# Attention with top-32 masking and routed experts on one core: a new order of emission, and value products of the shared tile that alternate between the heads

## The chip, the core and the metric

The kernel runs on one core of one Trainium2 chip. A core has TensorE (PE in the profile; its weight loads are shown as PEld), VectorE (DVE), ScalarE (ACT), GpSimd (POOL) and SyncE (SP), which here issues DMAs. Each engine works off its own queue of instructions in the order in which the program emitted them, and waits on semaphores for the others. The metric is device microseconds of one execution, here the median of three runs.

## The reference

For 8 batches of 8 heads, with 576 rows of 64, attention keeps for each row the scores that are not below the 32nd largest:

```python
scores = scale * np.matmul(q, k.transpose(0, 1, 3, 2))
kth = np.partition(scores, -top_k, axis=-1)[..., -top_k:-top_k + 1]
mask = scores >= kth
scores = np.where(mask, scores, -1000000000.0)
...
attn = attn / (np.sum(attn, axis=-1, keepdims=True) + 1e-09)
return np.matmul(attn, v).astype(np.float32)
```

Its output, 4608 tokens of 512, goes through a router with 8 experts. Tokens are assigned greedily by descending logit, each expert takes at most 576, and each expert is a product with w1, a ReLU and a product with w2.

## The kernel before, in words

The kernel has two parts, one behind the other: `attention` and `moe`. Only `attention` is touched by the change. It works through 32 pairs of heads (8 batches with 4 pairs each). A pair has 9 tiles of 128 query rows: tiles 0 to 3 are of the first head, 5 to 8 of the second, and tile 4, the shared tile, holds the last 64 rows of both heads, one on partitions 0 to 63 and one on 64 to 127.

One tile goes through this chain. TensorE forms scores in PSUM tile `s` (L216, four matmuls; three such tiles exist). VectorE takes the eight largest of each of six chunks of 96 (L219), and from these 48 candidates the 24 largest in five steps (L222 to L226: MAX, MATCH_REPLACE, MAX, MATCH_REPLACE, MAX). L227 forms a bias from the 24th, ScalarE writes a sign mask `w` and its count (L231). TensorE adds `w` times a huge number into `s` (L234 with `off`, a matmul of 512 columns and one of 64), before which VectorE fills 8 spare columns (L237). VectorE finds the next eight, ranks 25 to 32 (L238). TensorE takes the huge number out again (L234 with `back`), and ScalarE's ReLU turns scores into the mask tile `r` (L241), which frees `s` for the tile after the next two.

A second chain, later in time, goes from `r` to the output. TensorE lays mask and scores into PSUM tile `pt`, keys on partitions (L279, L284, L285), ScalarE takes the exponential `F` (L289), and GpSimd splits it into two fp16 halves, `ehm` (L292) and `elm` (L295). The value products (L363) sum these against `vh` and `vl`, twelve fp16 matmuls for each tile and one fp32 matmul for the last 64 keys (`E4`). The shared tile is not split: each head of it has four fp32 matmuls with `E` and one with `E4r`, with a weight of 64 columns, so that head 0 writes partitions 0 to 63 of `pv` and head 1 partitions 64 to 127. VectorE forms row sums and their reciprocal (L343, L377), ScalarE scales (L345).

Once for each pair GpSimd prepares the operands of a coming pair: q and k are scaled (L175), cut into high and low halves (L177, L178, L179), v is scaled (L167, L168), ScalarE makes its high half `vh` (L169), and GpSimd the low half `vl` (L170). SP issues the loads (L156, L157, L162, L163) and four transposing DMAs, K2, K3, Q2 and Q1 (L184), before the first scores of that pair may start. Three small transposes a pair (L266) bring the row maxima, which GpSimd prepares (L263 to L265). GpSimd also copies the pair's thresholds once (L307), which is used below as a mark for the end of a pair.

The order of all this is set by a list scheduler that runs while the program is built. `attention` hands `Plan.at` each operation with the ones that it needs, an assumed duration `d`, an assumed delay `late`, and a due time taken from the table `O`. `Plan.run` (L48 to L94) keeps a clock for each engine. For each engine it finds the operation that could start first, looks at all that could start within a window `WIN` behind it, and takes of these the one with the earliest due time:

```python
first = min(x[0] for x in can)
x = min((x for x in can if x[0] <= first + self.window[e]), key=lambda x: x[1])
if best is None or x[0] < best[0]: best = x
```

So the numbers in `O`, in `WIN` and in the durations decide nothing but the order in which each engine gets its instructions.

## Time and profile before

| what | value |
|---|---|
| three runs, median | 1432.83 us (1427.86 to 1434.24) |
| profiled execution, its own time | 1433.21 us |
| its span, first to last instruction | 1431.5 us |
| busy: TensorE, VectorE | 1281.9 us (90%), 1175.8 us (82%) |
| busy: ScalarE, GpSimd | 867.0 us (61%), 868.5 us (61%) |
| mean granted clock of TensorE | 0.977 of full speed |

The attention part runs until about 945 us, the experts from there to the end. Busy time is a union of recorded spans. A matmul's end is modelled and lies later than the moment at which the next one may start, and a VectorE record also runs on for some time after the next instruction has begun. So a share of 93% does not mean that the engine could take only 7% more work. What an instruction takes from its engine is better seen in the distance from its start to the next start.

### The profile page before, as it was taken

To read this page: it belongs to the slowest core of one execution; us is meant where nothing else is said; L and a number is where in the kernel's file an instruction comes from. 1 tells how busy PE (TensorE), PEld (TensorE's weight loads), DVE (VectorE), ACT (ScalarE), POOL (GpSimd) and SP (SyncE) were. 2 spreads that over 40 slices of the span, in tenths; PEclk is the share of its full clock that TensorE was granted. 3 is DMA by queue.
4 is the path that set the end of the run, shared out by engine and by line. 5 is a ranking of instruction groups with operands and counts; after the bars stand their busy time and mean duration, and the time that the engine had idled before them with its cause. 6 is when DMAs were issued, how large, how long until landed. Compare 5 with 4: busy or idle time off the path is not lost. (4 is left out here: it accounts for less than half of the span.)

```text
span 1431.5 us, 40890 instructions
## 1 busy us (share of the span) xinstructions
PE 1281.9 (90%) x14734; PEld 901.7 (63%) x14735; DVE 1175.8 (82%) x5815; ACT 867.0 (61%) x1906; POOL 868.5 (61%) x1285
## 2 busy tenths in 40 slices
PE   2889999999999999999999999948999899998995
PEld 1666776776767677776766777735566465564662
DVE  5899999999999999999999999858877867867620
ACT  2677777777777777787778778715433424424420
POOL 5787888798799789879878888611313303203201
PEclk9999999999999999999999999968999999999998
DMA  5434444444345444463445443004545726639301
GB/s 123 91 87 78 109 100 87 106 84 105 77 113 94 87 116 79 91 119 87 84 109 95 84 112 71 13 34 151 181 150 106 203 90 144 166 91 282 96 19 36
DMA packets 293381, 148.42 MB, mean 104 GB/s; under 512 B 250672, under 2 KB 275248, under 8 KB 292144
## 3 DMA queue, kind: packets, MB, share of 16 engines
q1 hardware_dynamic: 287280, 126.84, 39.2%
q0 software_dynamic: 5888, 18.88, 4.4%
q8 instruction: 117, 1.92, 0.6%
q14 instruction: 96, 0.79, 0.2%
HBM read 71.34 MB, written 18.87 MB: 63 GB/s over the span
## 5 line engine op out<-in xcount | busy, mean ns | idle before, releaser
L219 DVE MAX8 cd<-s 128x8 f32<-128x96 f32 x1728 | 372.9, 251 | 33.3 <-PE s L216 28.7
L295 POOL TENSOR_TENSOR elm<-F,ehm 128x512 f16<-128x512 f32 x256 | 294.4, 1156 | 7.9
L241 ACT ACTIVATE r<-s,st 128x576 bf16<-128x576 f32 x288 | 212.9, 739 | 105.8 <-PE s L234 72.0
L231 ACT ACTIVATE w<-s,st 128x576 uint16<-128x576 f32 x288 | 213.3, 740 | 80.3 <-DVE st L227 77.3
L971 POOL DMA_INDIRECT out_dram<-ob,idx x40 | 52.5, 1312 | 295.7 <-ACT ob L962 245.2
L238 DVE MAX8 st<-s 128x8 f32<-128x584 f32 x288 | 220.6, 766 | 7.5 <-PE s L234 2.8
L216 PE MATMUL s<-K,Q 128*128 128x512 f16 (+3 forms) x1280 | 192.2, 290 | 27.6 <-DMA Q<-nq 20.1
L928 PE MATMUL ph<-xT,w1h 128*128 128x288 f16 x1024 | 199.7, 294 | 16.5 <-DMA xT<-xs 16.5
L285 PE MATMUL pt<-Q,K 66*128 66x128 f16 (+1 forms) x1280 | 178.4, 215 | 0.0
L284 PE MATMUL pt<-Q,K 128*128 128x128 f16 (+1 forms) x1280 | 177.5, 215 | 0.0
L292 POOL TENSOR_SCALAR ehm<-F 128x512 f16<-128x512 f32 x256 | 156.6, 618 | 31.1 <-ACT F L289 28.6
L216 PEld LDWEIGHTS <-Q 128*128 128x128 f16 (+1 forms) x1280 | 104.6, 103 | 107.7 <-DMA Q<-nq 19.7
L234 PE MATMUL s<-w,off 128*128 128x512 f16 x576 | 132.4, 287 | 38.3 <-DVE s L237 29.1
L289 ACT ACTIVATE F<-pt 128x512 f32<-128x512 f32 x256 | 150.6, 596 | 14.0 <-PE pt L285 6.9
L928 PE MATMUL ph<-xT,w1l 128*128 128x288 f16 x512 | 150.2, 293 | 0.0
L363 PE MATMUL pv<-vt,E 128*64 128x65 f32 (+1 forms) x1024 | 146.7, 257 | 0.3 <-DVE L L414 0.3
L937 ACT ACTIVATE hh<-ph 128x288 f16<-128x288 f32 x128 | 52.2, 410 | 153.3 <-PE ph L928 146.5
L234 PE MATMUL s<-w,back 128*128 128x512 f16 x576 | 118.7, 288 | 20.9 <-DVE st L238 18.5
L284 PEld LDWEIGHTS <-K 128*128 128x128 f16 x1280 | 116.9, 98 | 18.4 <-issue 5.6
L928 PEld LDWEIGHTS <-w1h 128*128 128x128 f16 x1024 | 96.5, 100 | 44.8 <-issue 13.7
L363 PEld LDWEIGHTS <-ehm 128*128 128x128 f16 x2048 | 115.9, 101 | 9.8
L363 PEld LDWEIGHTS pv<-vt,E 128*64 128x64 f32 (+1 forms) x1024 | 113.1, 164 | 13.5 <-issue 3.1
(279 smaller groups left out, 3212.6 us busy)
## 6 DMA issues: line engine op xcount, KB each, us to landing
wr<-in_moe_w_dram SPq DMA_DIRECT2D x32, 1024.0 KB, 9.0
kn<-in_k_dram SPq DMA_DIRECT2D x64, 128.0 KB, 2.6
qn<-in_q_dram SPq DMA_DIRECT2D x64, 128.0 KB, 2.3
vn<-in_v_dram SPq DMA_DIRECT2D x64, 128.0 KB, 2.4
x<-xb SPq DMA_DIRECT2D x8, 1024.0 KB, 5.0
Q<-nq SPq DMA_TRANSPOSE x160, 3.3
...
```

Of the source, the lines that this page charges most:

```text
L216: T.matmul(s_ps[rows,a:b_],P[Q][:,qc],P[K][:,h*576+a:h*576+b_],start=(Q=="Q1"),stop=(Q=="Q2"))
L219: V.max(D["cd"][:,c*8:c*8+8],D["s"][:,576*c//NCH:576*(c+1)//NCH])
L231: A.activation(D["w"],D["s"][:,:576],AF.Sign,bias=P["st"][:,i,32:33],scale=(1+2.0**-21),accum_out=acc[:,col])
L234: T.matmul(D["s"][:,a:b_],by,w[:,a:b_],start=False,stop=True,skip_group_check=True)
L238: def next8(): V.max(P["st"][:,i,24:32],D["s"][:,:584])
L241: A.activation(r,D["s"][:,:576],AF.Relu,bias=P["st"][:,i,31:32],scale=-1.0)
L284: T.matmul(o,K2[:,kb:kb+128],Q1[:,qc],start=False,stop=False,skip_group_check=True)
L285: T.matmul(o,K3[0:66,kb:kb+128],Q2[0:66,qc],start=False,stop=(c==3 and h==sub[-1][0]),skip_group_check=True)
L292: G.tensor_scalar(D["eh"],D["E"],1.0,0.0,op0=ALU.mult,op1=ALU.add)
L295: G.tensor_tensor(el,D["E"],D["eh"],op=ALU.subtract); P["e"][i]=(D["eh"],el)
L363: for m_ in (range(N-1) if part==0 else (N-1,)): T.matmul(out,seq[m_][0],seq[m_][1],start=(m_==0),stop=(m_==N-1))
L928: P.matmul(B["ph"][:,:288],a[:,c,fs],xT[:,b+c,cs],start=(i==0),stop=(i==11))
```

## The change

Each instruction that was there before is there afterwards, in the same number on each engine. Two things differ. The first is the input of the list scheduler: the due times `O`, the windows `WIN`, and some assumed durations, among them those of the transposing DMAs (0.7 and 2.7 become 1.33 and 3.2) and of the value products. The second is `dot`, which emits the value products of the shared tile: it went through head 0 and then head 1, as two operations with two parts each, and now goes through the chunks with both heads in turn, as one operation with two parts. Lines behind L363 move down by two.

```diff
-        WIN={'V': 0.021, 'A': 0.06, 'G': 0.042, 'P': 0.137, 'D': 1.95}
+        WIN={'V': 0.029, 'A': 0.129, 'G': 0.076, 'P': 0.054, 'D': 2.18}
...
-        O=dict(ld=-6.228, hk=-184.89, hq=130.709, gk=-90.727, gk2=60.181, gq=-228.057, gq2=-152.349, tk=0.243, tk3=-91.804, tq=-142.303, lv=-11.274, hv=38.46, gv=95.514, gv2=69.183, S=-84.368, c0=138.764, c1=8.708, c2=131.547, c3=-93.268, c4=29.143, c5=127.672, nt=64.874, wb=-5.722, k0=-4.066, k1=-3.871, k2=-126.742, k3=-61.661, k4=49.194, nb=-24.073, sg=-141.852, wm=-4.889, y8=-122.303, j8=66.548, rl=-5.964, m1=-4.702, m2=-27.578, q2=25.46, t0=38.32, t1=41.765, t2=-1.545, td=-6.206, ex=119.352, eh=49.097, el=50.056, u0=32.63, ud=-33.856, ue=-89.992, uh=80.662, ul=-52.16, x0=27.529, xe=-46.133, xh=-94.111, xl=2.321, v0=42.098, v1=51.606, v2=42.831, vd=-2.418, vn=-72.153, vs=32.724, lg=54.377, lgd=7.08, l1=-156.701, l2=13.394, l3=-50.998, hg=-26.51)
+        O=dict(ld=1147.99, hk=113.989, hq=-226.905, gk=391.996, gk2=-589.556, gq=350.61, gq2=-1646.05, tk=-2028.85, tk3=109.327, tq=-1903.51, lv=2142.87, hv=-31.835, gv=-103.283, gv2=927.113, S=-1927.87, c0=2918.6, c1=-1296.6, c2=1489.31, c3=-1327.31, c4=-1779.83, c5=1141.95, nt=-30.266, wb=-1857.17, k0=-1815.22, k1=-1009.11, k2=-1615.05, k3=-591.96, k4=1985.52, nb=2679.75, sg=-577.738, wm=-828.345, y8=1389.73, j8=1687.45, rl=-305.088, m1=-1765.28, m2=1267.3, q2=-1079.71, t0=-229.078, t1=3079.77, t2=-966.324, td=146.127, ex=1259.47, eh=684.018, el=-263.634, u0=-1321.3, ud=-403.161, ue=-3285.38, uh=-584.173, ul=7.064, x0=-961.52, xe=62.633, xh=-833.718, xl=1370.57, v0=651.064, v1=1496.89, v2=706.436, vd=-293.21, vn=98.355, vs=-1103.64, lg=2045.55, lgd=3595.62, l1=-708.967, l2=-1227.56, l3=4081.72, hg=1783.46)
...
-            lk=at(t0+O["ld"],lambda: loads("k",k),o2,e="D",d=2.2,late=2.0); l=at(t0+O["ld"]+.01,lambda: loads("q",q),[lk],e="D",d=2.2,late=2.0)
+            lk=at(t0+O["ld"],lambda: loads("k",k),o2,e="D",d=2.3,late=3.0); l=at(t0+O["ld"]+.01,lambda: loads("q",q),[lk],e="D",d=2.3,late=3.0)
...
-            a=at(t0+O["tk"],lambda: turn("K2"),[h1]+p2,e="D",d=.7,late=2.7); b_=at(t0+O["tk3"],lambda: turn("K3"),[a,k2],e="D",d=.7,late=2.7)
+            a=at(t0+O["tk"],lambda: turn("K2"),[h1]+p2,e="D",d=1.33,late=3.2); b_=at(t0+O["tk3"],lambda: turn("K3"),[a,k2],e="D",d=1.33,late=3.2)
...
-                    av=D["av"]; vt,vh,vl=P["vt"],P["vh"],P["vl"]
-                    h=0 if g==0 else 1
-                    if g!=1: e_=P["e"][j if h==0 else 5+j]; out=av[:,j,:]; cs=lambda c: slice(c*128,c*128+128); last=P["e4"][:,j*128:j*128+128]
-                    else: h=j; e_=P["e"][4]; out=av[h*64:h*64+64,0,:]; cs=lambda c: slice(c*128+h*64,c*128+h*64+64); last=P["e4r"]
-                    if type(e_) is tuple: seq=[(e_[x][:,cs(c)],v_[:,h,c,:]) for c in range(4) for (x,v_) in ((0,vh),(0,vl),(1,vh))]
-                    else: seq=[(e_[:,cs(c)],vt[:,h*5+c,:]) for c in range(4)]
-                    seq.append((last,vt[:,h*5+4,:])); N=len(seq)
-                    for m_ in (range(N-1) if part==0 else (N-1,)): T.matmul(out,seq[m_][0],seq[m_][1],start=(m_==0),stop=(m_==N-1))
+                    av=D["av"]; vt,vh,vl=P["vt"],P["vh"],P["vl"]; runs=[]
+                    for h in ((0,1) if g==1 else (0 if g==0 else 1,)):
+                        if g!=1: e_=P["e"][j if h==0 else 5+j]; o_=av[:,j,:]; cs=lambda c: slice(c*128,c*128+128); last=P["e4"][:,j*128:j*128+128]
+                        else: e_=P["e"][4]; o_=av[h*64:h*64+64,0,:]; cs=lambda c,h=h: slice(c*128+h*64,c*128+h*64+64); last=P["e4r"]
+                        if type(e_) is tuple: seq=[(e_[x][:,cs(c)],v_[:,h,c,:]) for c in range(4) for (x,v_) in ((0,vh),(0,vl),(1,vh))]
+                        else: seq=[(e_[:,cs(c)],vt[:,h*5+c,:]) for c in range(4)]
+                        runs.append((o_,seq+[(last,vt[:,h*5+4,:])]))
+                    N=len(runs[0][1])
+                    for m_ in (range(N-1) if part==0 else (N-1,)):
+                        for o_,seq in runs: T.matmul(o_,seq[m_][0],seq[m_][1],start=(m_==0),stop=(m_==N-1),skip_group_check=(g==1))
...
-                for j in range(2 if g==1 else 4):
+                for j in range(1 if g==1 else 4):
...
-                        p=at(t0+O["vd"]*cnt,lambda j=j,part=part,dot=dot: dot(j,part),[p]+need,take="pt" if j==0 and part==0 else None,e="P",d=.224 if part else .36 if sp else .9); cnt+=1
+                        p=at(t0+O["vd"]*cnt,lambda j=j,part=part,dot=dot: dot(j,part),[p]+need,take="pt" if j==0 and part==0 else None,e="P",d=((.14 if part else .5) if g==1 else .14 if part else .38 if sp else .56)); cnt+=1
```

Left out here are changes of other assumed durations, of the same kind.

VectorE, about the 137th tile of 288, before. `s_10174` is tile 136 and `s_10226` tile 137, `cd` are the candidates and `st` the ranks of the pair.

```order
L222 MAX st_9335<-cd_10252 128x8 [waits DVE_49]
L237 TENSOR_SCALAR s_10174<-tab_168,acc_62 128x8 [waits Activation_49]
L223 MATCH_REPLACE cd2_10312<-st_9335,cd_10252 128x48 [waits DVE_49]
L224 MAX st_9335<-cd2_10312 128x8 [waits DVE_49]
L225 MATCH_REPLACE cd2_10312<-st_9335,cd2_10312 128x48 [waits DVE_49]
L238 MAX st_9335<-s_10174 128x8 [waits PE_49]
L226 MAX st_9335<-cd2_10312 128x8 [waits DVE_49]
L227 SCALAR_TENSOR_TENSOR st_9335<-s_10226,st_9335 128x1 [waits DVE_49]
L219 MAX cd_10365<-s_10348 128x8 [waits PE_49]
L219 MAX cd_10365<-s_10348 128x8 x3
L237 TENSOR_SCALAR s_10226<-tab_168,acc_62 128x8 [waits Activation_49]
L219 MAX cd_10365<-s_10348 128x8 x2
```

Here the steps L223, L224, L225 for one tile stand one behind the other, each needing the one before it. VectorE at the same tiles, with the change (`s_10171` is tile 136, `s_10217` tile 137):

```order
L237 TENSOR_SCALAR s_10149<-tab_168,acc_62 128x8 [waits PE_49]
L222 MAX st_9483<-cd_10241 128x8 [waits DVE_49]
L226 MAX st_9483<-cd2_10229 128x8
L223 MATCH_REPLACE cd2_10274<-st_9483,cd_10241 128x48 [waits DVE_49]
L227 SCALAR_TENSOR_TENSOR st_9483<-s_10171,st_9483 128x1 [waits DVE_49]
L238 MAX st_9483<-s_10149 128x8 [waits PE_49]
L224 MAX st_9483<-cd2_10274 128x8 [waits DVE_49]
L225 MATCH_REPLACE cd2_10274<-st_9483,cd2_10274 128x48 [waits DVE_49]
L237 TENSOR_SCALAR s_10171<-tab_168,acc_62 128x8 [waits Activation_49]
L226 MAX st_9483<-cd2_10274 128x8 [waits DVE_49]
L227 SCALAR_TENSOR_TENSOR st_9483<-s_10217,st_9483 128x1 [waits DVE_49]
L238 MAX st_9483<-s_10171 128x8 [waits PE_49]
```

The ranking of tile 137 is now mixed with the last rank of tile 136 (L226 behind L222) and its bias (L227 behind L223). At the end of the group of three the rows L226, L227, L238, L237 stand close together. Over all 288 tiles, the places at which one of L222 to L227 stands directly behind the row that it needs number 541 before (128 at L222, 110 at L223, 84 at L224, 113 at L225, 28 at L226, 78 at L227) and 245 with the change (75, 0, 0, 74, 31, 65).

GpSimd, where the values of a pair are prepared (`vt` scaled, `vl` its low half), before:

```order
L167 TENSOR_SCALAR vt1_195<-vn_9579 128x2x4x64 [waits PE_49]
L168 TENSOR_SCALAR vt1_195<-vn_9579 64x64 [waits DMAHW5_49]
L168 TENSOR_SCALAR vt1_195<-vn_9579 64x64 [waits PE_49,Pool_49]
L170 TENSOR_TENSOR vl1_201<-vt1_195,vh1_199 128x8x64 [waits Activation_49,Pool_49]
L292 TENSOR_SCALAR ehm_10667<-F_10637 128x512 [waits Activation_49]
L295 TENSOR_TENSOR elm_10685<-F_10637,ehm_10667 128x512 [waits Pool_49]
L292 TENSOR_SCALAR ehm_10731<-F_10712 128x512 [waits Activation_49]
L295 TENSOR_TENSOR elm_10754<-F_10712,ehm_10731 128x512 [waits Pool_49]
```

The row L170 stands directly behind L168 in 25 pairs of 32. The same with the change:

```order
L167 TENSOR_SCALAR vt1_195<-vn_9972 128x2x4x64 [waits DMAHW3_49,DMAHW1_49,PE_49]
L168 TENSOR_SCALAR vt1_195<-vn_9972 64x64 [waits DMAHW2_49,PE_49]
L168 TENSOR_SCALAR vt1_195<-vn_9972 64x64 [waits DMAHW4_49,PE_49,Pool_49]
L292 TENSOR_SCALAR ehm_10642<-F_10507 128x512 [waits Activation_49,Pool_49]
L175 TENSOR_SCALAR sc_10650<-kn_10142 128x576 [waits DMAHW2_49,DMAHW7_49,DMAHW1_49,DMAHW0_49]
L295 TENSOR_TENSOR elm_10667<-F_10507,ehm_10642 128x512 [waits Pool_49]
L292 TENSOR_SCALAR ehm_10691<-F_10542 128x512 [waits Activation_49]
L295 TENSOR_TENSOR elm_10706<-F_10542,ehm_10691 128x512 [waits Pool_49]
L170 TENSOR_TENSOR vl1_201<-vt1_195,vh1_199 128x8x64 [waits Activation_49]
L263 TENSOR_SCALAR m3_10757<-st_9483 128x3 [waits DVE_49]
```

Between L168 and L170 there are now other rows, mostly exponentials being split; L170 stands directly behind L168 in 8 pairs of 32, and in 22 pairs five or more rows stand between. The last L179 of a pair, on which the transpose Q1 waits, stands 15 to 17 rows ahead of the next L307 in the pairs of the middle, before 14 to 19.

TensorE, value products of the shared tile, before. `E4` closes the last full tile; `pv_9873` belongs to the shared tile.

```order
L363 MATMUL pv_9775<-vt1_195,E4_9588 128x65
L363 MATMUL pv_9873<-vt1_195,E_9496 64x65 [waits PE_49,Activation_49]
L363 MATMUL pv_9873<-vt1_195,E_9496 64x65 x3
L234 LDWEIGHTS off_164
L234 MATMUL s_9719<-w_9871,off_164 128x512 [waits DVE_49]
L234 LDWEIGHTS off_164
L234 MATMUL s_9719<-w_9871,off_164 128x64
L363 MATMUL pv_9873<-vt1_195,E4r_9654 64x65
L363 MATMUL pv_9873<-vt1_195,E_9496 64x65 x4
```

Head 0 comes first (L363 with `E_9496`, four), the closing matmul with `E4r` later, and then head 1. With the change:

```order
L365 MATMUL pv_9864<-vt1_195,E4_9598 128x65
L234 LDWEIGHTS off_164
L234 MATMUL s_9789<-w_9924,off_164 128x512 [waits DVE_49]
L234 LDWEIGHTS off_164
L234 MATMUL s_9789<-w_9924,off_164 128x64
L365 MATMUL pv_9961<-vt1_195,E_9411 64x65 x8
L365 MATMUL pv_9961<-vt1_195,E4r_9646 64x65 x2
L216 LDWEIGHTS Q1_9390
```

The eight matmuls with `E` now stand together, head 0 and head 1 in turn, and so do the two with `E4r`. The two `off` matmuls of a tile stand together in all 288 tiles, before in 216.

## Rows read from the trace of the kernel before

**Rows 1.** The windows view, two stretches of the span (us from its start): busy time and number of instructions of each engine, TensorE's granted clock, DMA share, GB/s.

```profile
60.00:930.00 870.00, 806.99 (x11083) 610.32 (x11080) 812.08 (x4656) 672.48 (x1561) 727.45 (x1127) 1.00 0.45 92
930.00:1431.50 501.50, 444.85 (x3395) 273.17 (x3392) 324.80 (x925) 170.22 (x297) 104.48 (x88) 0.94 0.44 125
```

**Rows 2.** The view of line L307, GpSimd's copy that marks the end of a pair (duration in ns, first and last start in us), and three of its instances in GpSimd's timeline (start us, us).

```profile
L307 POOL TENSOR_SCALAR cuts<-st x32: 202/213/218, 53.0 to 930.6; 128x9 f32<-128x9 f32 x32
...
450.73 0.21 POOL L307 TENSOR_SCALAR cuts<-st 128x9 f32<-128x9 f32 x1
...
477.23 0.21 POOL L307 TENSOR_SCALAR cuts<-st 128x9 f32<-128x9 f32 x1
...
507.50 0.21 POOL L307 TENSOR_SCALAR cuts<-st 128x9 f32<-128x9 f32 x1
```

**Rows 3.** The waits view of 60 to 860 us: which engine and line waited for which, us in total, times, longest.

```profile
ACT w L231 <- DVE st L227: 62.3, 109, 1.4
ACT r L241 <- PE s L234: 59.9, 95, 1.6
...
POOL vl L170 <- ACT vh L169: 46.6, 22, 2.9
...
PE s L234 <- DVE s L237: 23.3, 52, 1.0
...
DVE cd L219 <- PE s L216: 12.1, 35, 0.5
```

**Rows 4.** VectorE's timeline (start us, us, in brackets the idle time before it), first rows that need the one before them, then rows of two tiles mixed.

```profile
510.84 0.21 DVE L224 MAX8 st<-cd 128x8 f32<-128x48 f32 x1
511.08 0.09 DVE L225 MATCH_VALUE_LOAD cd<-st,cd 128x8 f32 x1
...
511.95 0.20 DVE L226 MAX8 st<-cd 128x8 f32<-128x48 f32 x1
512.18 0.16 DVE L227 SCALAR_TENSOR_TENSOR st<-s,st 128x1 f32<-128x1 f32 x1
512.41 0.92 DVE L219 MAX8 cd<-s 128x8 f32<-128x96 f32 x5
513.25 0.22 DVE L237 TENSOR_SCALAR s<-tab,acc 128x8 f32<-128x8 f32 x1
513.38 0.26 DVE L219 MAX8 cd<-s 128x8 f32<-128x96 f32 x1
513.67 0.21 DVE L222 MAX8 st<-cd 128x8 f32<-128x48 f32 x1
...
514.66 0.07 DVE L223 MATCH_VALUE_LOAD cd<-st,cd 128x8 f32 x1
...
514.83 0.26 DVE L219 MAX8 cd<-s 128x8 f32<-128x96 f32 x1
515.00 0.20 DVE L224 MAX8 st<-cd 128x8 f32<-128x48 f32 x1
515.11 0.25 DVE L219 MAX8 cd<-s 128x8 f32<-128x96 f32 x1
...
516.05 0.14 DVE L227 SCALAR_TENSOR_TENSOR st<-s,st 128x1 f32<-128x1 f32 x1
516.11 0.26 DVE L219 MAX8 cd<-s 128x8 f32<-128x96 f32 x1
...
517.90 0.21 DVE L237 TENSOR_SCALAR s<-tab,acc 128x8 f32<-128x8 f32 x1
...
518.42 0.76 DVE L238 MAX8 st<-s 128x8 f32<-128x584 f32 x1
519.10 0.14 DVE L343 TENSOR_SCALAR rs<-pv 128x4 f32<-128x4 f32 x1
```

**Rows 5.** GpSimd's timeline (as rows 4) behind the preparation of values in one pair.

```profile
496.30 1.16 POOL L170 TENSOR_TENSOR vl<-vt,vh 128x512 f16<-128x512 f32 x1 [1.13 <-ACT vh L169]
501.02 0.20 POOL L263 TENSOR_SCALAR m<-st 128x3 f32<-128x3 f32 x1 [3.56 <-DVE st L222]
```

**Rows 6.** TensorE's timeline with forms kept apart: value products of a shared tile; then, from the timeline of all engines, scores of a shared tile (eight matmuls with 64 columns of weights, heads in turn) and of a full tile (four).

```profile
410.59 0.27 PE L363 MATMUL pv<-vt,E4r 128*64 128x65 f32 x1
410.60 0.27 PE L363 MATMUL pv<-vt,E 128*64 128x65 f32 x1
...
410.71 0.57 PE L363 MATMUL pv<-vt,E 128*64 128x65 f32 x7
...
513.89 0.68 PE L216 MATMUL s<-K,Q 128*64 128x512 f16 x8
...
516.03 0.65 PE L216 MATMUL s<-K,Q 128*128 128x512 f16 x4
```

**Rows 7.** SP's timeline: the last transpose (Q1) before pair 17; the landing times of L184 between 400 and 700 us; and the first scores of pair 17 in the timeline of all engines.

```profile
494.92 1.31 SPq L184 DMA_TRANSPOSE Q<-nq  x1
...
DMA to landing us min/median/max: 3.3/3.9/4.9
...
502.78 0.65 PE L216 MATMUL s<-K,Q 128*128 128x512 f16 x4
```

More of the change, by code (lines that the diff above doesn't have):

```diff
@@ L247, in tile_ops @@
             for m in range(5):
-                p=at(t0+O["k%d"%m],lambda m=m: rank(m),p if m==0 else [p],e="V",d=.18 if m%2 else .11)
+                p=at(t0+O["k%d"%m],lambda m=m: rank(m),p if m==0 else [p],e="V",d=.187 if m%2 else .11)
                 if m==0: P["mx"][i]=p
-            p=at(t0+O["nt"],minus,[p],e="V",d=.065)
-            p=at(t0+O["sg"],sign,[p],e="A",d=0.717)
-            f_=at(t0+O["j8"],fill,[p],e="V",d=0.12)
+            p=at(t0+O["nt"],minus,[p],e="V",d=.075)
+            p=at(t0+O["sg"],sign,[p],e="A",d=0.732)
+            f_=at(t0+O["j8"],fill,[p],e="V",d=0.125)
             p=at(t0+O["wm"],lambda: move(off,0),[p],e="P",d=0.216)
@@ L266, in q2 @@
                 def q2(): nc.sync.dma_start_transpose(P["Q2t"][:,i0:i0+3,:],P["nq"][:,1,i0:i0+3,:].rearrange("p a b -> p (a b)"))
-                a=at(t0+O["m1"],most,[P["mx"][j] for j in range(i0,i+1)],e="G",d=.6); P["q2"][i0//3]=at(t0+O["q2"],q2,[a],e="D",d=.65,late=2.0)
+                a=at(t0+O["m1"],most,[P["mx"][j] for j in range(i0,i+1)],e="G",d=.75); P["q2"][i0//3]=at(t0+O["q2"],q2,[a],e="D",d=1.22,late=2.7)
         def soft(P,i):
@@ L378, in values @@
                 p=at(t0+O["vd"]*cnt+O["vn"],sums,[p],e="V",d=.07); p=at(t0+O["vd"]*cnt+O["vn"]+.05,inv,[p],e="V",d=.09)
[L379 removed]
+                for j in range(n_): p=at(t0+O["vd"]*cnt+O["vs"],lambda D=D,j=j,dst=dst: scale(D["av"],D["r"],j,dst()),[p],free=[tp] if j==n_-1 else None,e="A",d=.225)
                 last.append(p)
@@ L401, in piece @@
                 p=tp=at(t,turn,[done],take="pt",e="P",d=.11*len(turns))
-                p=tx=at(t+O["l1"],copy,[p],free=[tp],take="xT",e="A",d=.06+w*.00083)
+                p=tx=at(t+O["l1"],copy,[p],free=[tp],take="xT",e="A",d=.115+w*.00083)
                 p=tp=at(t+O["l2"],dot,[p],take="pt",free=[tx],e="P",d=.224*len(turns))
-                fin.append(at(t+O["l3"],lambda: put(D["lg"]),[p],free=[tp],e="V",d=.08))
+                fin.append(at(t+O["l3"],lambda: put(D["lg"]),[p],free=[tp],e="V",d=.1))
             main=L[:,b*4:b*4+4,:]; last=L[o:o+64,32+b//2,:]
```

25 lines of the change are left out of this document (12 added, 13 removed).

## The prediction

> **What bounds the kernel now.** I read the busy windows first. Over 60 to 930 us, where attention runs, TensorE is busy 806.99 of 870 us, VectorE 812.08 and GpSimd 727.45: 93%, 93% and 84% [rows 1]. No engine stands out, and TensorE has its full clock of 2.4 GHz there. Behind 930 us the experts take 501.5 us; the change moves nothing there, so I leave them and the 1.7 us around the span as they are.
>
> The second view is the line of GpSimd's once-a-pair copy. 32 of them start between 53.0 and 930.6 us, so a pair takes (930.6 - 53.0)/31 = 28.3 us [rows 2]. Pairs differ: one takes 26.5 us (450.73 to 477.23), the next 30.3 us (to 507.50). With the same work in both, the order in which it stands is worth 3.8 us for a pair.
>
> The third view is the waits. They are many and small: ScalarE waits 62.3 us for VectorE's bias and 59.9 us for the closing matmul, GpSimd 46.6 us in 22 pieces for `vh`, TensorE 23.3 us for the fill, VectorE 12.1 us for scores [rows 3]. So this is a ring of five queues, each of which waits now and then for the one ahead of it.
>
> The last view is VectorE's timeline, where I take the distance from start to start as the price of an instruction [rows 4]. A chunk maximum costs 0.165 us (five in 0.92, of which the last is 0.26 long), a MATCH_REPLACE with its value load 0.17 (514.66 to 514.83), a maximum over 48 mixed with another tile 0.11 (515.00 to 515.11), the bias 0.06 (516.05 to 516.11), the fill 0.13 (513.25 to 513.38), the maximum over 584 0.68 (518.42 to 519.10). A tile has 6, 2, 3, 1, 1 and 1 of these: 0.99 + 0.34 + 0.33 + 0.06 + 0.13 + 0.68 = 2.53 us, a pair 22.8 us. Where a step stands directly behind the one that it needs, it starts later: 0.24 in place of 0.11 behind L224 (510.84 to 511.08), 0.23 in place of 0.11 behind L226 (511.95 to 512.18), 0.29 in place of 0.165 behind a chunk (513.38 to 513.67). The surcharge is 0.12 to 0.13 us.
>
> **VectorE's order.** 541 such places become 245, 296 fewer. At 0.12 us that is 35 us of VectorE's queue, 1.1 us a pair. Before, a pair needs 22.8 + 541/32 x 0.12 = 24.8 us, and with nine small rows for the row sums (some 0.5 us, an estimate from the prices above) 25.3; the other 3.0 of the 28.3 us are waits. With the change the need is 24.2 us. How much of the 35 us shortens the run depends on whether VectorE was waited for there: between 0 (it reaches its next wait earlier and stands there) and 35. VectorE issues for 25.3 of 28.3 us, near nine tenths, so I take the upper half and say two thirds: -23 us.
>
> The Trainium skill speaks against this term. Its page VectorE: DVE Perf Modes, section The DRAIN you can't avoid, says that each VectorE instruction waits for the pipeline to empty whether or not it needs the one before, that a semaphore between them adds nothing, and it advises to cut the number of operations and not the semaphores. By that rule 296 fewer dependent neighbours are worth 0. The rows above differ: 0.11 us between independent maxima and 0.24 between dependent steps. I go by the rows, and give the rule a share in the first rival.
>
> **GpSimd's order.** L170 right behind L168 makes GpSimd wait for ScalarE's `vh`: 46.6 us in 22 pieces, 2.1 us each [rows 3]. In one pair the next wait follows, 3.56 us for ranks [rows 5]. 25 such places become 8, so 17 x 2.1 = 36 us of GpSimd's waiting goes. Its worth lies between 0 and 36. GpSimd is busy for 727.45/870 x 28.3 = 23.7 us of a pair, so it can catch up behind most of these waits, and the split exponentials of pairs ahead lie ready for TensorE in 14 buffers. I take a quarter: -9 us. What is late next is GpSimd's own wait for ranks and exponentials.
>
> **Value products of the shared tile.** Eight fp32 matmuls of one head run as 16 records 0.058 us apart (seven in 0.57 with the last 0.22 long, divided by six) [rows 6]. A pair has ten fp32 matmuls, 20 records: 1.17 us. Where head 0's `E4r` and head 1's first `E` are neighbours, they start 0.01 us apart [rows 6], so the two halves of the array work at once. The scores of the shared tile alternate already, and their eight matmuls take 0.68 us against 0.65 for the four of a full tile [rows 6], half for each. So alternation saves 0.58 us a pair, 19 us in all on TensorE. Before and after, ScalarE's ReLU and VectorE's ranks decide when TensorE may go on, so its worth lies between 0 and 19; I take a quarter, -5 us.
>
> **What the new order gives back.** At the end of each group of three tiles stand L226, L227, L238 (one tile back), L237, and then chunks. From a fill (517.90) to the L238 of its tile (518.42) at least 0.52 us pass [rows 4], since TensorE's `off` lies between. Before, ranks lie in that gap; now only L226 and L227 with one surcharge do: 0.13 + 0.11 + 0.12 + 0.06 = 0.42. That is 0.1 us three times a pair, 0.3 x 31 = +9 us; 0 at best. Also, `off` matmuls stand together in all tiles, before in 216, so in 72 tiles TensorE now stands in front of the second one until the fill has come. The wait of that kind took 23.3 us in 52 pieces, 0.45 each [rows 3]: 0 to 72 x 0.45 = +32 us. TensorE's queue has value products and masks that can be late without harm, so I put it at 0 here and use the upper end for a rival. New due times for loads and transposes cost nothing as long as they land ahead: for pair 17 Q1 is issued at 494.92 and lands within 3.3 to 4.9 us, the scores start at 502.78, so 3 us or more are left [rows 7].
>
> **Sum.** -23 - 9 - 5 + 9 = -28 us, 27.4 us for a pair. The profiled execution took 1433.21 us, 0.4 over the median of the three: 1433 - 28 = 1405 us. With all lower ends it is -35 - 36 - 19 = -90, but GpSimd's 23.7 us and VectorE's 24.2 us with any waits at all forbid that; the fastest pair seen, 26.5 us, would be 31 x 1.8 = 56 us less.
>
> **Rivals.** First, no change: the time saved on VectorE is waited away, because each tile's chain of scores, ranks, mask, ranks, unmask and ReLU goes through three `s` tiles, and a pair can be no shorter than that chain. For it: ScalarE's 59.9 us behind TensorE and 62.3 us behind VectorE [rows 3] are waits inside that chain. Against it: pairs of 26.5 us exist with the same three tiles [rows 2]. If the skill's rule on VectorE held, it would end here too. It leaves -9 - 5 + 9: 1428 us.
>
> Second, all pairs run like the best one. For it: the new order repeats every three tiles on VectorE, and GpSimd's preparation is spread evenly, where the old one had it in a block. Against it: one in four pairs carries the router's extra products. 1433 - 56 = 1377 us.
>
> Third, slower: TensorE stands in front of `off` and holds the scores of the next tile and the unmasking behind it. Its price is 72 x 0.45 = 32 us. It decides if the third of rows 3 grows from 23.3 to 50 us or more while VectorE's need falls into waits: 1433 - 9 - 5 + 32 = 1451 us. Against it: before the change such waits were hardly passed on, VectorE waited 12.1 us for scores.
>
> Fourth, the change does not do what it says for the shared tile: alternation gives no overlap, because the two heads' matmuls into one `pv` tile are not let run together. Then the -5 us are missing: 1410 us. The two starts 0.01 us apart speak against it, and it would not change the sign.
>
> **Chances.** The forecast with the fourth rival 0.54, no change 0.18, all pairs like the best 0.15, slower 0.13. Half a per cent, 7 us, is about what a measurement of this kernel can tell from no change. The forecast's own range is 1390 to 1422 us. Faster by more than that: 0.54 + 0.15 and a little of the second case that is within: 0.69. Same: 0.17. Slower: 0.14. The whole range goes from 1384 (VectorE's 35 us in full and the other gains as taken, 35 + 9 + 5 = 49 us, nothing given back) to 1438 us (no change, and 5 us of spread between runs as in the three shown), which leaves out the slower case and the end of the best one.
>
> **What would show it.** L307 should again start 32 times, the last near 903 us; pairs of 27.4 us on average, more alike than 26.5 and 30.3. VectorE's busy time in attention falls by some 10 to 20 us (part of the surcharge is recorded as busy), GpSimd's wait at L170 falls from 46.6 to about 15 us, and the ten shared products stand in some 0.6 us. The experts keep their 501.5 us. The prediction is wrong if a pair still takes over 28 us; then VectorE's wait for `w` or for scores, or TensorE's for the fill, must have grown by what the 296 places gave.

## The result: slower by 0.9%

The kernel after the change takes 1446.09 us in the median of four runs (1443.12 to 1446.27). The kernel before took 1433.18 us on the same chip. The ratio is 1.0093, with a 95% interval of 1.0065 to 1.0121, so the change costs about 13 us where I had forecast a gain of 28. The profiled execution, the fastest of the four, took 1443.12 us with a span of 1441.2, which is 9.7 us more than before.

Line numbers behind L363 are two higher now (L365 for L363, L415 for L413, L422 for L420).

**Where the time went.** The last write to the router's logits splits the span. First VectorE's timeline of the kernel before:

```profile
943.92 0.17 DVE L420 TENSOR_TENSOR L<-lg,L 64x8 f32<-64x8 f32 x1 [0.34 <-PE lg L408]
```

and of the kernel after:

```profile
966.57 0.17 DVE L422 TENSOR_TENSOR L<-lg,L 64x8 f32<-64x8 f32 x1 [0.34 <-PE lg L410]
```

Attention ends 22.65 us later. What follows takes 1441.2 - 966.7 = 474.5 us in place of 1431.5 - 944.1 = 487.4, 12.9 us less, although no instruction of it changed. So 22.6 us lost and 12.9 us won make the 9.7 us of the span.

**The pace of attention.** L307, GpSimd's mark, answers to [rows 2]:

```profile
L307 POOL TENSOR_SCALAR cuts<-st x32: 207/212/219, 53.1 to 947.9; 128x9 f32<-128x9 f32 x32
```

A pair takes (947.9 - 53.1)/31 = 28.86 us; it was 28.31. A steadier mark is ScalarE's ReLU (L241), one for each tile. Of its 288 instances these are the 37th and the 253rd before, from ScalarE's timeline:

```profile
143.40 0.74 ACT L241 ACTIVATE r<-s,st 128x576 bf16<-128x576 f32 x1 [0.21 <-PE s L234]
...
821.33 0.74 ACT L241 ACTIVATE r<-s,st 128x576 bf16<-128x576 f32 x1 [0.21 <-PE s L234]
```

and after, the 37th, 109th, 145th, 217th and 253rd:

```profile
146.91 0.75 ACT L241 ACTIVATE r<-s,st 128x576 bf16<-128x576 f32 x1
...
377.17 0.75 ACT L241 ACTIVATE r<-s,st 128x576 bf16<-128x576 f32 x1
494.76 0.75 ACT L241 ACTIVATE r<-s,st 128x576 bf16<-128x576 f32 x1
...
724.87 0.75 ACT L241 ACTIVATE r<-s,st 128x576 bf16<-128x576 f32 x1
839.37 0.75 ACT L241 ACTIVATE r<-s,st 128x576 bf16<-128x576 f32 x1
```

24 pairs took 677.9 us and take 692.5: four pairs 113.0 and 115.4. The four pairs from 724.87 to 839.37 take 114.5, those from 377.17 to 494.76 take 117.6. No stretch at the lower clock lies in the first of these two and 10.2 us of them lie in the second, so I put the difference down to TensorE's clock (below). So the steady period grew by 1.5 us for four pairs, 12 us over the whole, and some 5 us are stretches at the lower clock. The rest of the 22.6 us lies at the ends: the first ReLU starts at 30.4 us in place of 27.7, and from the last ReLU to the last logits 3.2 us more pass.

The same marks give the steady period of every kernel without the clock. Of the 24 pairs only those count that no half-clock stretch (below) touches. They are averaged for each of the four places that a pair can have in its batch, and the four averages are added. By this, four pairs take 112.99 us before and 114.47 after. In the new order the third place has only one or two such pairs. The table of experiments has this sum for all kernels.

**The engines did no more, and waited more.** The page's first part, busy time over the whole span, of the kernel before:

```profile
PE 1281.9 (90%) x14734; PEld 901.7 (63%) x14735; DVE 1175.8 (82%) x5815; ACT 867.0 (61%) x1906; POOL 868.5 (61%) x1285
```

and after:

```profile
PE 1277.7 (89%) x14734; PEld 890.0 (62%) x14735; DVE 1156.1 (80%) x5815; ACT 868.0 (60%) x1906; POOL 873.0 (61%) x1285
```

With the same instructions VectorE is busy for 19.7 us less. The windows view from the 37th to the 253rd ReLU holds the same 24 pairs in both kernels, before

```profile
143.40:821.33 677.93, 630.47 (x8653) 476.29 (x8652) 634.51 (x3643) 524.76 (x1219) 574.44 (x889) 1.00 0.47 96
```

and after:

```profile
146.91:839.37 692.46, 630.57 (x8653) 468.77 (x8652) 620.12 (x3643) 525.79 (x1220) 576.22 (x889) 0.98 0.46 94
```

VectorE is busy for 14.4 us less there (634.51 to 620.12) and idle for 28.9 us more (43.4 to 72.3), which together is the 14.5 us by which these pairs take longer. The windows view of 60 to 930 us after the change answers to [rows 1]; there VectorE went from 812.08 to 777.31 us, but from 4656 to 4562 instructions too, since attention now reaches further behind 930 us:

```profile
60.00:930.00 870.00, 790.71 (x10847) 587.25 (x10844) 777.31 (x4562) 657.44 (x1523) 721.10 (x1111) 0.98 0.45 92
```

What VectorE saved came back as waits. The waits view of 60 to 860 us, after (compare [rows 3]):

```profile
ACT r L241 <- PE s L234: 120.2, 142, 1.7
ACT w L231 <- DVE st L227: 29.8, 85, 1.1
...
POOL ehm L292 <- ACT F L289: 54.4, 55, 2.9
...
POOL vl L170 <- ACT vh L169: 6.9, 6, 1.2
...
DVE st L238 <- PE s L234: 23.8, 84, 0.4
DVE cd L219 <- PE s L216: 20.5, 70, 1.3
DVE s L237 <- ACT w L231: 13.6, 41, 0.4
DVE rs L343 <- PE pv L365: 4.7, 28, 0.2
...
PE s L234 <- DVE s L237: 29.7, 88, 0.4
```

and four rows of the same view before, which I had not shown:

```profile
POOL ehm L292 <- ACT F L289: 21.2, 36, 1.5
...
DVE s L237 <- ACT w L231: 6.3, 24, 0.4
DVE rs L343 <- PE pv L363: 0.8, 4, 0.2
...
DVE st L238 <- PE s L234: 0.3, 2, 0.2
```

VectorE's four waits sum to 62.6 us after and, with 12.1 for scores [rows 3], to 19.5 before: 43 us more, which is more than the saving. ScalarE's ReLU waits twice as long for TensorE. The wait that I expected to shrink did (`vl` 46.6 to 6.9 us), and ScalarE's wait for VectorE's bias halved as well (62.3 to 29.8). The largest of the four, that of L238 for `off` (0.3 to 23.8 us), is the gap of a group's close that I had priced at 9 us.

VectorE's timeline shows such a close of three tiles:

```profile
503.93 0.19 DVE L224 MAX8 st<-cd 128x8 f32<-128x48 f32 x1
504.16 0.09 DVE L225 MATCH_VALUE_LOAD cd<-st,cd 128x8 f32 x1
504.24 0.19 DVE L225 MATCH_REPLACE8 cd<-st,cd 128x48 f32<-128x48 f32 x1
504.47 0.21 DVE L226 MAX8 st<-cd 128x8 f32<-128x48 f32 x1
505.08 0.23 DVE L237 TENSOR_SCALAR s<-tab,acc 128x8 f32<-128x8 f32 x1 [0.40 <-ACT w L231]
505.22 0.15 DVE L227 SCALAR_TENSOR_TENSOR st<-s,st 128x1 f32<-128x1 f32 x1
505.81 0.78 DVE L238 MAX8 st<-s 128x8 f32<-128x584 f32 x1 [0.44 <-PE s L234]
506.50 0.21 DVE L237 TENSOR_SCALAR s<-tab,acc 128x8 f32<-128x8 f32 x1
506.91 0.59 DVE L219 MAX8 cd<-s 128x8 f32<-128x96 f32 x3 [0.20 <-PE s L216]
```

At 505.08 us all three `s` tiles are past their first 24 ranks and none is through its ReLU, so there is little that VectorE could do: it waits for the mask, for `off` and for the next scores, 1.04 us in one group. A saving ahead of such a place only brings VectorE there sooner.

**TensorE's clock.** Windows of the kernel after: a stretch, the one behind it, and one of the experts.

```profile
219.00:223.40 4.40, 2.84 (x40) 1.89 (x37) 4.25 (x32) 3.71 (x9) 3.55 (x7) 1.00 0.40 77
223.40:226.90 3.50, 2.99 (x11) 1.23 (x11) 2.78 (x11) 2.20 (x4) 3.23 (x4) 0.51 0.39 103
...
1326.00:1332.80 6.80, 3.05 (x13) 1.90 (x14) 2.67 (x4) 2.21 (x4) 1.33 (x1) 0.50 1.22 277
```

and, from TensorE's timeline, what stands ahead of the second:

```profile
222.97 0.41 PE L234 MATMUL s<-w,back 128*128 128x512 f16 x2 [0.97 <-DVE st L238]
```

From 219.0 to 223.4 us TensorE was busy for 2.84 of 4.40 us, with a wait of 0.97 us at the end, and then the granted clock was half, 1.2 in place of 2.4 GHz. Of such stretches between 60 and 930 us the new order has eight, 3.4 or 6.8 us long, and the old one none [rows 1, clock 1.00]. Seven of the eight begin within 3 us of the end of such a wait of 0.97 us; the old order has waits of up to 1.02 us in the same line and no stretch behind them, so the wait alone is not the cause. Six of the eight come once in each batch of four pairs, 116 us apart (107.4, 223.4, 339.5, 455.6, 571.6 and 687.7 us). Behind the last logits it is the other way round: the experts had four half-clock stretches before, 20.4 us long together, and have one of 6.8 us now. Over the traces of this study the part behind the logits takes 474.5 to 477.5 us where these stretches sum to 6.8 us (three traces), 479.5 to 486.0 with 10.2 or 13.6 us, and 487.4 and 487.7 with 20.4.

The clock is not all of the 12.9 us, though. The sum of the windows view over the four stretches before is

```profile
sum 20.40, PE 17.70 PEld 11.16 DVE 7.29 ACT 3.35 POOL 3.92; mean PE 4.43 PEld 2.79 DVE 1.82 ACT 0.84 POOL 0.98
```

At half the clock 17.7 us of TensorE hold work for 8.9 us at the full one, and the 3.05 us after work for 1.5: my estimate is 7.3 us for the clock. TensorE's waits for the experts' input (`xT`) got shorter too, by the profile's page of before

```profile
L928 PE MATMUL ph<-xT,w1h 128*128 128x288 f16 x1024 | 199.7, 294 | 16.5 <-DMA xT<-xs 16.5
```

and after:

```profile
L930 PE MATMUL ph<-xT,w1h 128*128 128x288 f16 x1024 | 193.2, 288 | 12.1 <-DMA xT<-xs 12.1
```

That is 4.4 us. From the start of GpSimd's last write of results to the end of the span 15.2 us passed before (1416.33 to 1431.5) and 13.0 pass now (1428.20 to 1441.2), 2.2 us. These three sum to 13.9 us, of which other pieces took back 1. Why the waits and the last write became shorter stays open.

### The profile page after: what moved, and what is told of

Its sections match the earlier page's. It is cut to its first block, busy times and chain, and to the rows that moved or that the text cites. A ratio compares the mean times of both kernels' runs of the same rounds, so it can differ in the third digit from the quotient of the medians.

```text
span 1441.2 us, 41199 instructions
## 1 busy us (share of the span) xinstructions
PE 1277.7 (89%) x14734; PEld 890.0 (62%) x14735; DVE 1156.1 (80%) x5815; ACT 868.0 (60%) x1906; POOL 873.0 (61%) x1285
## 5 line engine op out<-in xcount | busy, mean ns | idle before, releaser
L219 DVE MAX8 cd<-s 128x8 f32<-128x96 f32 x1728 | 364.4, 251 | 43.5 <-PE s L216 39.2
L241 ACT ACTIVATE r<-s,st 128x576 bf16<-128x576 f32 x288 | 213.4, 741 | 154.4 <-PE s L234 138.8
L295 POOL TENSOR_TENSOR elm<-F,ehm 128x512 f16<-128x512 f32 x256 | 295.6, 1155 | 8.1
L238 DVE MAX8 st<-s 128x8 f32<-128x584 f32 x288 | 221.1, 768 | 28.6 <-PE s L234 28.0
L216 PE MATMUL s<-K,Q 128*128 128x512 f16 (+3 forms) x1280 | 198.1, 296 | 36.6 <-DMA Q<-nq 22.5
L973 POOL DMA_INDIRECT out_dram<-ob,idx x40 | 55.4, 1386 | 283.6 <-ACT ob L964 235.7
L930 PE MATMUL ph<-xT,w1h 128*128 128x288 f16 x1024 | 193.2, 288 | 12.1 <-DMA xT<-xs 12.1
L216 PEld LDWEIGHTS <-Q 128*128 128x128 f16 (+1 forms) x1280 | 108.1, 105 | 125.5 <-issue 34.3
L930 PE MATMUL ph<-xT,w1l 128*128 128x288 f16 x512 | 147.2, 288 | 0.0
L234 PE MATMUL s<-w,back 128*128 128x512 f16 x576 | 121.8, 294 | 17.2 <-DVE st L238 14.9
L365 PE MATMUL pv<-vt,E 128*64 128x65 f32 (+1 forms) x1024 | 128.1, 258 | 0.0
L284 PEld LDWEIGHTS <-K 128*128 128x128 f16 x1280 | 119.0, 99 | 12.9 <-issue 6.6
L365 PEld LDWEIGHTS <-ehm 128*128 128x128 f16 x2048 | 117.8, 102 | 7.9 <-issue 0.5
L279 PE MATMUL pt<-nid,r 128*128 128x128 bf16 (+1 forms) x1280 | 113.2, 215 | 9.2 <-DVE st L222 8.7
L365 PE MATMUL pv<-vh,ehm 128*128 128x65 f16 x1024 | 120.7, 195 | 0.5 <-ACT F L289 0.5
```

The source lines that it names most:

```text
L216: T.matmul(s_ps[rows,a:b_],P[Q][:,qc],P[K][:,h*576+a:h*576+b_],start=(Q=="Q1"),stop=(Q=="Q2"))
L219: V.max(D["cd"][:,c*8:c*8+8],D["s"][:,576*c//NCH:576*(c+1)//NCH])
L234: T.matmul(D["s"][:,a:b_],by,w[:,a:b_],start=False,stop=True,skip_group_check=True)
L238: def next8(): V.max(P["st"][:,i,24:32],D["s"][:,:584])
L241: A.activation(r,D["s"][:,:576],AF.Relu,bias=P["st"][:,i,31:32],scale=-1.0)
L284: T.matmul(o,K2[:,kb:kb+128],Q1[:,qc],start=False,stop=False,skip_group_check=True)
```

## Experiments

`us` in the table is the median and the ratio is to the kernel before on the same chip. The column `logits at` is the end of the last write to the logits in the profiled execution, which the clock in the experts does not touch. The last column is the sum of four pairs at the full clock, as above, which no half-clock stretch touches (in h2 and i1 one place of the four has no such pair).

| kernel | us | ratio, 95% interval | logits at | four pairs |
|---|---|---|---|---|
| before | 1433.18 | 1 | 944.1 | 112.99 |
| after | 1446.09 | 1.0093 [1.0065, 1.0121] | 966.7 | 114.47 |
| e1 new order, heads in sequence | 1455.69 | 1.0155 [1.0127, 1.0184] | 972.6 | 115.42 |
| e2 old order, heads alternate | 1431.05 | 1.0004 [0.9986, 1.0022] | 946.4 | 113.03 |
| f1 new, idle maxima at the close | 1446.63 | 1.0116 [1.0079, 1.0154] | 960.4 | 114.42 |
| f2 new, idle maxima in the middle | 1450.89 | 1.0135 [1.011, 1.0159] | 970.5 | 115.23 |
| g1 old, idle maxima in the middle | 1440.54 | 1.0058 [1.0035, 1.0081] | 954.2 | 114.05 |
| g2 old, idle maxima at the close | 1438.30 | 1.0061 [1.0039, 1.0083] | 953.9 | 113.92 |
| h1 new, tiles first on TensorE | 1452.84 | 1.0157 [1.0126, 1.0188] | 970.7 | 114.95 |
| h2 new, tiles first, ScalarE too | 1452.55 | 1.0143 [1.0118, 1.0167] | 971.8 | - |
| h3 old, tiles first | 1438.62 | 1.0055 [1.0036, 1.0075] | 956.8 | 113.98 |
| i1 new, no `vl` products | 1429.27 | 0.9976 [0.9953, 0.9999] | 946.1 | - |
| i2 old, no `vl` products | 1423.13 | 0.9947 [0.9921, 0.9973] | 935.5 | 111.98 |
| i4 new, no subtraction on GpSimd | 1450.39 | 1.0145 [1.0101, 1.0189] | 960.0 | 114.33 |
| p1 old priorities, new DMA times | 1467.24 | 1.025 [1.0213, 1.0288] | 984.0 | 117.54 |
| j1 new, TensorE busy at the start | 1450.05 | 1.0125 [1.0098, 1.0151] | 969.5 | 114.41 |
| j2 old, TensorE busy at the start | 1432.23 | 1.0008 [0.9994, 1.0021] | 946.1 | 112.96 |

**The two parts of the change apart (e1, e2).** e1 is the new order with one head's products behind the other's (the diff is to after), e2 the old order with the new loops and both heads' products where head 1's stood.

```diff
-for m_ in (range(N-1) if part==0 else (N-1,)):
-    for o_,seq in runs: T.matmul(o_,seq[m_][0],seq[m_][1],start=(m_==0),stop=(m_==N-1),skip_group_check=(g==1))
+for o_,seq in runs:
+    for m_ in (range(N-1) if part==0 else (N-1,)): T.matmul(o_,seq[m_][0],seq[m_][1],start=(m_==0),stop=(m_==N-1),skip_group_check=(g==1))
```

> The changed kernel with its new order kept row for row, but the shared tile's ten value products go through head 0 first and then head 1. Theory A (the order costs the time: VectorE's saved queue time falls into round trips through ScalarE and TensorE, and alternation is a small gain): the ten products take 1.2 us again in place of 0.6, and the time is that of the changed kernel or up to 10 us more, 1446 to 1456 us. Theory B (alternation costs the time, because TensorE has less to do and its clock is halved in attention): the stretches at half clock in attention go and the time falls to 1440 us or below.

> The kernel before with its order kept, except that the shared tile's products of both heads are emitted, alternating, where head 1's stood. Theory A: the order is the old one, so the time is that of before or a little less, 1423 to 1435 us. Theory B: TensorE's clock falls to half in places in attention, where it did not before, and the time rises by 5 us or more over 1433.

Measured: the new order alone is 1.5% slower, and alternation gives back 0.6% of it. In the old order alternation is worth nothing. The last column says the same: 2.4 us for four pairs by the order, of which alternation gives back 0.95, and 0 in the old order. It does what it says: in TensorE's timeline of after the 20 records of both heads start within 0.58 us (the last is 0.22 long), where [rows 6] led to 1.17 us.

```profile
424.81 0.69 PE L365 MATMUL pv<-vt,E 128*64 128x65 f32 x16
425.32 0.29 PE L365 MATMUL pv<-vt,E4r 128*64 128x65 f32 x4
```

In the old order TensorE waits most of that time away, 11.4 of some 16 us. The waits view of e2 over 60 to 860 us, against 23.3 and 14.1 us before:

```profile
PE s L234 <- DVE s L237: 30.8, 52, 1.3
...
PE s L234 <- DVE st L238: 18.0, 35, 1.1
```

**What VectorE's time is worth (f1, f2, g1, g2).** 96 maxima over 96 columns of a constant, 0.165 us each and 16 us in all, into a tile that nobody reads; once ahead of L238 of tiles 1, 4 and 7 (the close: f1, g2), once among the chunk maxima of tiles 2, 5 and 8 (the middle: f2, g1).

```diff
+def idle(): V.max(wk.tile([128,8],F32,tag="idle",name="idle",bufs=4),identf[:,0:96])
...
 def next8():
+    if i%3==1: idle()
     V.max(P["st"][:,i,24:32],D["s"][:,:584])
...
     V.max(D["cd"][:,c*8:c*8+8],D["s"][:,576*c//NCH:576*(c+1)//NCH])
+    if i%3==2 and c==3: idle()
```

> The changed kernel with an idle maximum over 96 values on VectorE right ahead of the maximum over 584 of every third tile (the second of each group of three), 96 in all, some 0.165 us each, 16 us of VectorE's queue. Theory A: VectorE waits there anyway for the round trip of the fill through TensorE (23.8 us in 84 places in the profile), so the added work costs little: 0 to 5 us over the changed kernel's 1446. If VectorE's queue sets the end: 16 us more, 1462.

> The same 96 idle maxima, placed among the chunk maxima of the third tile of each group, where VectorE does not wait in the profile. Theory A: it is paid there in full or nearly, 10 to 16 us over 1446, since the close of the group comes later by as much. If VectorE has slack everywhere: as in the other place, 0 to 5 us.

> The old order with 96 idle maxima over 96 columns on VectorE (0.165 us each, 16 us) among the chunk maxima of every third tile, where in the new order they cost 4.8 us of the 16. If VectorE's sum of work sets the pace in the old order (the step of my prediction that turned two thirds of its time into span): 1432 + 11 = 1443 or more. If the round trips set it there as well: 1432 + 0 to 6.

> The old order with the 96 idle maxima (16 us of VectorE) ahead of the maximum over 584 columns of every tile 3k+1, where they cost 0.5 us in the new order. If VectorE holds the path at the close of a group in the old order: 1432 + 8 or more. If it waits there in the old order too: 1432 + 0 to 4.

Measured: in the old order the 16 us cost 0.58% and 0.61%, 8 to 9 us, wherever they stand, and the logits come 10 us later. In the new order they cost 0.42% over after in the middle (6 us, the logits 3.8 us later) and 0.2% at the close, within the error, while the logits come 6 us earlier (between the 37th and the 253rd ReLU its trace has four half-clock stretches, that of after six). At the close they fell into a wait. f1's waits view has (its line numbers are higher by the added lines)

```profile
DVE cd L220 <- PE s L217: 16.1, 61, 0.4
...
DVE st L241 <- PE s L235: 7.9, 30, 0.3
```

The wait for `off` went from 23.8 to 7.9 us, by the 16 us put ahead of it. g2, the old order with the same maxima in the same place, had nothing there that could take them:

```profile
DVE cd L220 <- PE s L217: 8.9, 25, 0.5
...
DVE st L241 <- PE s L235: 0.6, 3, 0.2
```

The last column agrees, without the clock. Four pairs hold 2.0 us of these maxima. In the old order they cost 1.1 and 0.9 us, in the new one nothing at the close and 0.8 in the middle (115.23 against 114.47). So VectorE's time was worth about half its length before, wherever it stood. After, it is worth nothing at the close of a group. In the middle it is worth little less than before, and the intervals of the times don't tell that apart.

**A repair of the queues (h1, h2, h3).** The trace of after shows scores of 104 tiles behind products of the softmax and of the values on TensorE, and 33 signs behind an exponential on ScalarE. These kernels put them ahead. The planner is left as it is; its list is edited before it is emitted.

```diff
+loom.ahead={("S",5):0.29,("S1",5):0.29,("S",12):0.44,("S1",12):0.44,
...
+m=self.ahead.get((op.get("k"),op.get("tile")))
+if m:
+    l=L[op["e"]]; i=l.index(op); l.pop(i)
+    while "tile" not in l[i-1] and l[i-1]["d"]<=m+.1 and l[i-1] not in op["pre"]: m-=l[i-1]["d"]; i-=1
+    l.insert(i,op)
```

> The new order with TensorE's queue edited alone: where the trace of after shows the scores of a tile (104 tiles, 39.2 us of products of other work in front of them that began when the scores could already have run) or its off pair (20 tiles, 5.9 us) behind products of the softmax or of the values, they are put ahead of as much of that work. The work itself is the same. Theory A (what the new order lost are round trips of the s tiles, which wait in queues behind other work): three tiles share a period, so up to 45.1/3 = 15 us come back, 1446 to between 1431 and 1440. Rival B (the pace is TensorE's sum of work, or GpSimd's chain of exponentials): 1446 +- 3, since the products put behind are late instead. Rival C (the half clock in short stretches is what costs): the time follows the count of such stretches, about ten in attention now, and falls by no more than 6 us.

> The same edit of TensorE's queue, and on ScalarE the sign of 33 tiles (20.6 us late behind an exponential) ahead of that exponential. Theory A: (39.2 + 5.9 + 20.6)/3 = 22 us at most, 1446 to between 1424 and 1436, and below the run with TensorE alone. Rival B: 1446 +- 3; a worse one, 1450 and more, if exponentials that come later starve GpSimd (its wait for F, 54 us in after, would grow).

> The same rule used on the old order, by the trace of before: scores of 56 tiles (17.3 us), off pairs (19 tiles 6.7 us, 10 second halves 2.4 us), back pairs (36 tiles, 10.1 us) and signs (35 tiles, 11.3 us) ahead of other work. Theory A: at most 47.8/3 = 16 us, 1432 to between 1416 and 1428. Rival B: 1432 +- 3.

Measured: all three are slower, by 0.5 to 0.6%. So pulling ahead the tiles that stand behind other work, the repair by theory A, does not bring the loss back; another choice of tiles was not tried. The waits view of h1 shows what happened (L379 is L343 here, L401 is L365):

```profile
POOL ehm L328 <- ACT F L325: 59.9, 66, 3.1
...
DVE cd L255 <- PE s L252: 14.8, 41, 0.4
...
DVE rs L379 <- PE pv L401: 12.5, 56, 0.5
```

The scores did come earlier (20.5 to 14.8 us), and what was pushed back was late in their place (row sums on value products 4.7 to 12.5, exponentials 54.4 to 59.9).

**What TensorE's time is worth (i1, i2).** The products of the low halves of the values are left out: their part of the output is missing.

```diff
-for (x,v_) in ((0,vh),(0,vl),(1,vh))
+for (x,v_) in ((0,vh),(1,vh))
```

> The new order with the products of the values' low halves (L365, vl with ehm, 1024 instructions some 0.031 us apart, 32 us of TensorE) left out, the order otherwise as it is. Theory T (in the new order the path runs over TensorE's queue more than over VectorE's): half of it or more comes back, 1446 to between 1422 and 1431. Rival R (the round trip of the s tiles through all engines paces it and no engine's sum does): below 8 us, 1438 or more.

> The same products left out of the old order. Theory T: the path runs over VectorE's queue there (a VectorE idle maximum cost 9 us of 16 in the old order, and 19 us of TensorE's shared products gave nothing), so less than a third comes back: 1432 to between 1421 and 1432, and clearly less than in the new order. If both orders gain the same, the bound has not moved between the engines.

Measured: the same 32 us of TensorE are worth 1.17% in the new order, 17 us, and the logits come 20.6 us earlier. In the old order they are worth 0.53%, 8 us, and the logits come 8.6 us earlier. By the last column they are worth 1.0 us of four pairs in the old order; in the new one each of the three places that can be compared gains 0.56 to 0.59 us for a pair, 2.3 us for four. Theory T stands: the bound has moved from VectorE towards TensorE. The rows fit it. If one follows the traces back from the 253rd ReLU to the 37th, at each step to what released an instruction by the profile or to the one ahead of it, TensorE has 46% of that chain before and 57% after, VectorE 41% and 35%.

**GpSimd (i4).** L295 is left out and the products use the high half twice. The first four chunks of keys weigh double against the fifth, whose exponentials are not split; the expectation overlooked that.

```diff
-el=wk.tile([128,512],F16,tag="elm",name="elm",bufs=PLANBUFS["eh"])
-G.tensor_tensor(el,D["E"],D["eh"],op=ALU.subtract); P["e"][i]=(D["eh"],el)
+P["e"][i]=(D["eh"],D["eh"])
```

> The new order with GpSimd's subtraction of the exponentials' halves left out (L295, 256 instructions of 1.16 us, 296 of GpSimd's 666 us of the steady part); the products read the high half twice instead, which scales the sums of a row with its values, so the output is nearly the same. GpSimd is not on the path by theory T and by R: 1446 +- 4. Rival G (the late exponentials, GpSimd's wait for F grown from 21 to 54 us, pace the new order): 1446 to 1430 or lower.

The windows view has GpSimd at 453.19 us of 870, against 721.10 in after:

```profile
60.00:930.00 870.00, 789.69 (x10940) 588.72 (x10937) 782.20 (x4600) 663.01 (x1536) 453.19 (x875) 0.99 0.46 92
```

Over a third of GpSimd's work gone gave no gain in the time. Its logits come 6.7 us earlier, as in f1, two hundredths of what was taken away, and four pairs at the full clock take 114.33 us against 114.47. GpSimd's longer wait for exponentials (54.4 us) is a symptom.

**The DMA times alone (p1).**

```diff
-lambda: turn("K2"),[h1]+p2,e="D",d=.7,late=2.7
+lambda: turn("K2"),[h1]+p2,e="D",d=1.33,late=3.2
...
```

> The old priorities, windows and compute durations, with the one thing that the title of the change names: the planner's times of the DMAs (transposes 0.7 to 1.33 us of issue and 2.7 to 3.2 us to landing, corrections 0.65/2.0 to 1.22/2.7, loads 2.2/2.0 to 2.3/3.0, stores 2.0 to 2.6), which moves instructions on all engines too. If the DMA times as such make the better order: below 1425. If they only stir an order whose priorities were found with other times: slower than before, 1435 to 1470. If they hardly matter to the pace: 1432 +- 4.

Measured: 2.5% slower. Truer times in the planner (of loads, small transposes and stores too, which are not shown above) are no gain by themselves. This is the second case of the expectation, though that the old priorities had been found with the old times is its reason and nothing that the run shows.

**The start (j1, j2).**

```diff
+warm=ps_t.tile([128,512],F32,tag="pt",name="warm")
+for _ in range(140): T.matmul(warm[:,0:128],nid60,nid60,start=True,stop=True)
 loom.run()
```

> The new order with 140 matmuls of nid60 on itself (128 columns, 0.06 to 0.11 us each, 8 to 15 us) on TensorE while it waits for the first loads and transposes (its first scores start at 22.5 us); their result is not read. They cost nothing if TensorE is through by then, and shift what TensorE did before the granted clock is set. If the half-clock stretches in attention cost what I read (0.5 to 1 us each, about 6 in all) and their places hang on the start: they move, and the time follows their count, 1440 to 1446. If the places stay as they are: 1446 +- 2.

> The same 140 matmuls ahead of the old order, whose matmuls run at the half clock at the start (128 columns in 0.107 us up to 37 us of the span, against 0.055 us later). If that start costs: 1432 to between 1425 and 1430, faster than both kernels. If attention's first 20 us wait for loads and VectorE anyway: 1432 +- 2.

Measured: nothing won in either. j1 has as many half-clock stretches from 100 to 930 us as after, seven, partly in other places, so what they cost stays read from the ReLU marks and was not shown by an experiment.

No version ran faster than the kernel before with the whole computation in it.

## Why the prediction was wrong, point by point

**VectorE's order, -23 us: the step that failed.** That VectorE would be relieved was right: 19.7 us of busy time went, at the upper end of the 10 to 20 that I named as the recorded part of 35. Two thirds as its price was not far off for the old order, where g1 and g2 give 0.53 to 0.55 by the ratios, 0.63 by the logits and 0.5 by the pairs at the full clock. But the price belongs to an order and to a place in it. The change replaced the order, and in the new one VectorE's time is worth 0.2 to 0.4 in the middle and nothing that can be measured at the close, where the three `s` tiles make it wait. What was taken from VectorE came back as 43 us of waits: for the same 24 pairs it was busy 14.4 us less and idle 28.9 us more (its waits grew by more than that, and the short gaps between its rows shrank). This is what the first rival said, that the saved time is waited away behind three `s` tiles; its 1428 us were still too low.

The Trainium skill's rule that I weighed against this term (VectorE: DVE Perf Modes, The DRAIN you can't avoid) would have made it 0 as I told it. I left out that the same section goes on to say that a next instruction which is not held starts earlier, so the rule in full need not make it 0. The rows still differ: L224 to L225 takes 0.23 us in the new order, too (503.93 to 504.16), against 0.11 between independent maxima [rows 4]. No gain came, but not for want of a saving, since VectorE's busy time did fall.

**What the new order gives back, +9 us: mis-sized.** I saw the close of three tiles and priced one gap, 0.1 us a group, and left out that L237 waits for the sign and the next chunks for scores as well. The group shown waits 1.04 us; the four waits of VectorE grew by 43 us over some 28 pairs, 1.5 us a pair, 0.5 us a group.

**GpSimd's order, -9 us: true of the wait, nothing on the path of the new order.** The wait fell from 46.6 to 6.9 us, further than to the 15 us that I named, and GpSimd waits for exponentials instead (21.2 to 54.4 us). i4 shows that GpSimd is not what sets the pace in the new order. What its time was worth in the old one was not tested.

**Alternation, -5 us.** The size on TensorE was right. Its worth is 0 in the old order and 0.6%, 9 us, in the new one, 6 us of it ahead of the logits: a third to a half of the 19 us. So the quarter that I took was right for neither.

**The third rival had the sign and the wrong mechanism.** Its mark was TensorE's wait for the fill growing from 23.3 to 50 us; it grew to 29.7.

**Pairs of 26.5 and 30.3 us: misread.** Between the first two marks of L307 in [rows 2] lie 8 ReLUs, between the next two 10. I took it for the same work. By the ReLU marks the old order's pairs from the 37th ReLU to the 253rd are all alike, 27.9 to 28.9 us, so the second rival had no ground, and neither had what I held against the first.

**What I kept constant was not.** The part behind attention became 12.9 us shorter, some 7 of them by TensorE's clock, and the first scores start at 22.53 us in place of 20.07, since the new list on SP puts loads between the first two transposes of Q. I had costed the new due times at nothing.

**What is settled and what is not.** Shown: the new order is what costs, not alternation; VectorE's time lost its price at the close of a group, and TensorE's price doubled; GpSimd's has none in the new order; pulling these tiles ahead makes it worse. Read from rows alone: the division of the 22.6 us into a longer steady period (12), the clock (5) and the two ends (6), and that of the 12.9 us behind it. Open: which engine's list does it. No run exchanged the list of one engine, or the priorities of one kind of operation, by itself. Why the clock falls where it does stays open too.
